# Side work of a unit in smaller pieces: reciprocal in quarters, head scaling and weight parts spread, down jobs shared out

## Chip, cores and metric

The kernel runs on one core of a Trainium2 chip. The metric is device microseconds of one execution. The kernel is one program for five engines, each with its own in-order queue: TensorE (PE, with its weight loads shown as PEld), VectorE (DVE), ScalarE (ACT), GpSimd (POOL) and SyncE (SP), the last two only issuing DMAs in the part that matters here.

## The reference

A gated mix of a linear-attention block and a bilinear feed-forward block over 2048 tokens of width 512, in float32:

```python
g = sigmoid((x * gate_w).sum(-1))
# a: 32 heads of width 16
q, k, v = x @ wqkv            # 512 x 1536
pq, pk = phi(q), phi(k)       # phi(t) = (t + 1 if t > 0 else exp(t)) + 1e-6
kv, z  = pk^T v, pk.sum(tokens)          # per head
a = (pq @ kv) / (pq . z + 1e-6) @ wo
# b: no nonlinearity, F = 1792
b = ((x @ w_gate) * (x @ w_up)) @ w_down
out = g * a + (1 - g) * b
```

## The kernel before

**Numbers in halves.** Every float32 operand of a large product is split into a high part (fp32r, a copy on ACT) and a low part (what is left, a subtraction on DVE), and a product is three matmuls (`mm3`): high x high, high x low, low x high. The split of a weight block `wr` gives `wch` (ACT) and `wcl` (DVE).

**Two passes.** The first pass (to about 95 us) computes k, phi(k) and x^T phi(k). The second, which the change touches, runs 32 *units*: two pairs of token chunks (`pair` 0 and 1, 2 x 512 tokens each) times 16 units. A unit of kind "f" makes 128 columns of gate and up together for both chunks; a unit of kind "q" makes the q of 16 heads (256 columns as two rows of 128) for both chunks. The order in a pair is f0 to f5, q0, f6 to f9, q1, f10 to f13, so q units are n = 6 and 11, and n = 22 and 27 in the second pair.

**A unit** replaces the eight 128 x 256 x 512 products of a 2 x 2 block product by seven (a Strassen form). The seven products of six matmuls each go to the four PSUM banks Y, X, R, S in the order 2 (Y), 3 (X), 4 (Y), 1 (R), 5 (X), 6 (R), 7 (S). Between them ACT and DVE combine: `m2` is Y copied by ACT; R = X - m2 (DVE); `cross[:, 0]` is Y copied by ACT; t = R + cross (DVE); S = t - X (DVE); `cross[:, 1]` is X copied by ACT. An "f" unit then multiplies the two halves on DVE (`cross`), and splits them into the *hidden* tiles `hh` (ACT) and `hl` (DVE). A "q" unit instead runs `quad` four times: exp and relu on ACT, a combine on DVE, into `phq`. m2 and t share one buffer name, so the profile calls m2 `m`.

**Side work in a unit.** A unit has places at which other work is put in the order of the program: (n, -1) after R, (n, 0) after the first `cross` copy, (n, 1) after S, (n, 2) at its end. `fill(place, k)` emits up to k *down jobs* from the list `jobs` and then all that was put at that place by `later`. A **down job** multiplies 128 tokens of two hidden tiles by their w_down blocks (six matmuls into PSUM tile `pdn`, two buffers), and DVE adds the scaled result to the output accumulator `acc`. Two f units give 8 jobs; a unit takes 1 + 1 + 2 while there are any. **Weights** of unit n+1 are split at (n, 1) by `up_weights` (three ACT copies, three DVE subtractions), followed by the negated copy for n+2 and POOL's accumulating DMA load; `w_load(n + 3)` follows the unit on SP. **down_weights** splits the unit's w_down block (`dh`, `dl`). In the first pair, 14 half tiles of the second pair's x sums are loaded, split (`cbs`) and parked in DRAM (`xpark`).

**The attention of one q unit n** is spread over later units: in n+1 the head sums (`z_parts`, `z_sum`) and the denominator (`evac` to `den`, 32 x 512); in n+2 its reciprocal in two halves (`recip`) and a DMA that spreads it to rows in DRAM (`spread`, `den<-den`); at the ends of n+2 and n+3 DMAs load four row blocks `rb` (`norm`); in n+3 and n+4 `norm2` multiplies them with phi(q) on DVE and splits them on ACT and DVE; in n+4 the folded weights kv @ wo are loaded from `wpark` (`weights`); `last` runs the head's 8 down jobs at one go, in unit n+5, or at the end of n+4 where the pair ends there.

**The turn.** After unit 15 SP reloads the x tiles from `xpark` (14 loads of 512 KB, in the order in which a unit's products use them), and PE runs all jobs that are left: 8 of f12 and f13, then 8 of q1. The same 16 end the program after unit 31; a finished tile of `out` is stored as soon as its accumulator is complete.

All PE, ACT, DVE, SP and POOL instructions named here keep their program order on their engine. Tile buffers are released in program order and waits follow from that.

Of the kernel before, what the change touches and what calls it, by code (L numbers as in the profile page):

```python
# [7 lines left out]
F32 = mybir.dt.float32  # L8
# [6 lines left out]
P = 128  # L15
# [28 lines left out]
def gated_mix(ctx: ExitStack, tc, xt, xp, x, wqkv, wq, wq_add, wo, wgu, wgu_add, wdn, gate_w, out):  # L44
# [12 lines left out]
    def act(dst, src, func=AF.Copy, **kw):  # L57
        pin(nc.scalar.activation(dst, src, func, **kw))  # L58

    def tt(dst, a, b, op):  # L60
        pin(nc.vector.tensor_tensor(dst, a, b, op=op))  # L61

    def stt(dst, a, scalar, b, op0, op1):
        pin(nc.vector.scalar_tensor_tensor(dst, a, scalar, b, op0=op0, op1=op1))  # L64

    def split(hi, lo, src, copy="act"):

        if copy == "act":
            act(hi, src)
        else:  # L70
            pin(nc.vector.tensor_copy(hi, src))
        tt(lo, src, hi.bitcast(F32), ALU.subtract)
# [72 lines left out]
            act(raws[n][:, 5:7], raws[n][:, 0:2], scale=-1.0)  # L145
            dma_add(raws[n][:, 2:7], (wgu_add if kind == "f" else wq_add)[m])

    def w_split(n, parts):
        if n < len(order):
            if n not in wcs:  # L150
                wcs[n] = [const.tile([P, 7, 2 * P], F32R, tag=f"wc{v}", name=f"wc{v}", bufs=2) for v in "hl"]
            for a, b in parts:
                split(wcs[n][0][:, a:b], wcs[n][1][:, a:b], raws[n][:, a:b])


    A1, A2, B1, B2 = range(4)
# [16 lines left out]
    with tc.tile_pool(name="p1", bufs=2, reuse_waits="tile") as p1:  # L173
# [119 lines left out]
        plan(14, lambda: w_split(0, ((0, 2), (2, 4))))  # L293
        plan(15, lambda: w_split(0, ((4, 7),)))
        plan(16, lambda: w_load(2))
        for t in range(LEAD, NT + LEAD):
            if t < NT:
# [34 lines left out]
    def later(n, place, fn):  # L332
        at.setdefault((n, place), []).append(fn)

    def fill(place, n):
        for fn in jobs[:n]:
            fn()
        del jobs[:n]
        for fn in at.pop(place, []):
            fn()  # L340

    def unit(w, n, quad):

        wh, wl = w
# [36 lines left out]
        if quad:  # L381
            quad(0, 0, bank["S"])
        else:
            hh, hl = hidden()
            act(hh[:, 1], cross[:, 1])
# [63 lines left out]
    def down_jobs(pair, group, col):  # L449

        def job(i):
            t = pair * TPP + i
            c, sl = divmod(i, CH // P)
            sl = slice(sl * P, (sl + 1) * P)
            pd = psum.tile([P, D], F32, tag="dn", name="pdn", bufs=2)
            for j, ((hh, hl), w2) in enumerate(group):
                mm3(pd, (hh[:, c, sl], hl[:, c, sl]), w2, j == 0, j == 1)
            s = col[:, t:t + 1]
            if (pair, i) not in acc:
                acc[pair, i] = p2.tile([P, D], F32, tag="acc", name="acc", bufs=8)  # L460
                act(acc[pair, i], pd, scale=s)
            else:
                a = acc[pair, i]
                stt(a, pd, s, a, ALU.mult, ALU.add)
            left[pair, i] -= 1
            if not left[pair, i]:
                to = nc.gpsimd if pair == 0 else nc.sync
                tc.keep_in_program_order(to.dma_start(out[t * P:(t + 1) * P, :], acc[pair, i]))
        return [lambda i=i: job(i) for i in range(TPP)]


    def attention(pair, j, n):
# [26 lines left out]
            den["d"] = p2.tile([4 * HB, CH], F32, tag="den", name="den")  # L499
            act(den["d"], den["p"], AF.Identity, bias=dcol[:, j, 0:1])  # L500

        def recip(half):
            sl = slice(half * CH // 2, (half + 1) * CH // 2)
            pin(nc.vector.reciprocal(den["d"][:, sl], den["d"][:, sl]))  # L504

        def spread():
# [7 lines left out]
            dma(rb, there[HB * i:HB * (i + 1)].rearrange("h j c -> (h j) c"))  # L514
            den[i] = rb

        def norm2(i):
            r, c = parts[i]
            rb = den[i]
            stt(rb, phs[r, c], EPS, rb, ALU.add, ALU.mult)  # L520
            split(group[r][0][0][:, c], group[r][0][1][:, c], rb)

        def weights():
            for r in range(2):
# [3 lines left out]
                group[r] = (group[r][0], d)  # L528

        def last():  # L530
            for fn in down_jobs(pair, [group[0], group[1]], gcol):
                fn()

        for i in range(4):
            later(n + 1, i // 2 - 1, lambda i=i: z_parts(i))
        for i in range(4):
            at.setdefault((n + 1, i // 2), []).insert(i % 2, lambda i=i: z_sum(i))
        later(n + 1, 1, evac)
        later(n + 2, -1, lambda: recip(0))
        later(n + 2, 0, lambda: recip(1))  # L540
        later(n + 2, 0, spread)
        for i, (m, place) in enumerate(((n + 3, 1), (n + 4, -1), (n + 4, 0), (n + 4, 1))):
            later(n + 2 + i // 2, 2, lambda i=i: norm(i))
            later(m, place, lambda i=i: norm2(i))
        later(n + 4, 0, weights)
        if n + 5 in (units, 2 * units):
            later(n + 4, 2, last)
        else:
            later(n + 5, 0, last)
        return quad  # L550


# [14 lines left out]

    wp_load()
    g_evac()
    later(0, 1, d_unit)  # L570
    later(1, 0, kv_unit)
    later(1, 1, lambda: wp_unit(0))
    later(1, 1, lambda: wp_unit(1))
    later(2, 0, lambda: wp_unit(2))
    later(2, 0, lambda: wp_unit(3))
    for n, (i, k) in enumerate((i, k) for i in (2, 3, 4, 1, 5, 6, 7) for k in range(2)):
        later(n, 1, lambda i=i, k=k: cb_load(i, k))
        later(n + 1, 0, lambda i=i, k=k: x_add(cb[i, k], 1, i, k))
        later(n + 2, 0, lambda i=i, k=k: cb_split(i, k))
    wdr = {}  # L580

    def d_load(n):
# [8 lines left out]
    for n, (pair, kind, m) in enumerate(order):  # L591
        entry = {}

        def down_weights(n=n, entry=entry):
            entry["d"] = down_tiles()
            split(*entry["d"], wdr.pop(n))
            d_load(n + 1)

        def up_weights(n=n):
            w_split(n + 1, ((0, 2), (2, 4), (4, 7)))  # L600
            w_add(n + 2)

        if kind == "f":
            at.setdefault((n, 0), []).insert(0, down_weights)
        at.setdefault((n, 1), []).insert(0, up_weights)
        quad = attention(pair, m, n) if kind == "q" else None
        hid = unit(wcs.pop(n), n, quad)
# [12 lines left out]
        fill((n, 2), len(jobs) if turn or n + 1 == len(order) else 0)  # L620


# [49 lines left out]
```

## Time and profile before

| | |
|---|---|
| timed runs, median of 3 | 649.72 us (648.67 to 650.14) |
| profiled execution, device time | 648.4 us |
| its span | 646.7 us |
| mean granted TensorE clock | 0.989 |
| second pass, start of unit 0 | about 95.9 us |
| end of the 16 jobs of the turn, start of unit 16 | 377.7 us |

A row of a timeline gives start, duration, engine, line, operation, the tiles written and read, shape and count; in brackets stands the engine's idle time just before it and what ended it. All helpers record one line each (52 for matmuls, 58 for ACT, 61 and 64 for DVE, 81 and 84 for DMAs), so groups are told apart by tiles. A row of waits gives who waited, for whom, total us, times, and the longest. A row of windows gives the stretch and its length, then busy time of PE, PEld, DVE, ACT and POOL with counts, the granted PE clock, the share of the DMA engines and GB/s. A row of a chain gives start, duration and work. A row of DMA issues gives size and us from issue to landing.

### The profile page before, as it was taken

How to read it: one execution, taken by the hardware profiler on the slowest of the kernel's cores; microseconds unless marked ns; L12 is line 12 of the kernel's file. 1: busy time of each engine (PE TensorE's matmuls, PEld its weight loads, DVE VectorE, ACT ScalarE, POOL GpSimd, SP SyncE). 2: the span in 40 equal slices, each digit the busy share in tenths (PEclk: the TensorE clock that was granted, in tenths of full speed). 3: DMA queues.
4: the chain of work that ended last, by engine and by line, in shares of the span. 5: the costliest groups of instructions: out<-in, count | busy, mean ns of one | idle time of the engine just before them, and what ended most of it. 6: DMA issues, size and time to landing. Idle time of an engine off the chain costs nothing.

```text
span 646.7 us, 7560 instructions
## 1 busy us (share of the span) xinstructions
PE 621.2 (96%) x2695; PEld 498.6 (77%) x2695; DVE 452.0 (70%) x693; ACT 295.4 (46%) x507; POOL 46.4 (7%) x62
## 2 busy tenths in 40 slices
PE   8999999999999899999897999999999999999997
PEld 5788887878888687787675877888887877877775
DVE  5977874555778868768778546457677786777764
ACT  2765754466456453445344025553365442553410
POOL 0011100001111100111100021000000100000000
PEclk9999999999999999999898899999999999999999
DMA  8477935578676797816986956553345763347203
GB/s 274 152 221 157 281 108 175 120 259 188 174 183 162 197 239 194 214 26 162 250 223 201 387 231 147 113 115 99 98 98 120 177 190 83 82 99 164 72 32 131
DMA packets 41926, 106.67 MB, mean 165 GB/s; under 512 B 4384, under 2 KB 6432, under 8 KB 41888
## 3 DMA queue, kind: packets, MB, share of 16 engines
q1 hardware_dynamic: 34480, 77.87, 37.6%
q0 software_dynamic: 7408, 28.32, 23.5%
q8 instruction: 21, 0.34, 0.2%
q14 instruction: 17, 0.14, 0.1%
HBM read 88.34 MB, written 17.83 MB: 164 GB/s over the span
## 4 chain that ended last, share of the span: by engine, by line
PE 77%; DVE 14%; ACT 4%; issue 2%; DMA 2%; SPq 0%; DVEq 0%
PE pdn L52 27%; PE bY L52 11%; PE bX L52 10%; PE bR L52 10%; PE gt L52 6%; PE pk L52 6%; PE bS L52 5%; DVE wcl L61 3%; ACT hh L58 3%; DVE hl L61 2%; DVE acc L64 2%; DVE rb L64 2%; DVE den L504 1%; DMA wr<-in_wgu 1%; PE pd L52 1%
## 5 line engine op out<-in xcount | busy, mean ns | idle before, releaser
L52 PE MATMUL pdn<-dh,hh 128*128 128x512 f32 x288 | 113.5, 394 | 7.8 <-ACT hh L58 7.8
L64 DVE SCALAR_TENSOR_TENSOR acc<-pdn,ocol,acc 128x512 f32<-128x512 f32 x96 | 71.7, 750 | 63.4 <-PE pdn L52 62.6
L52 PE MATMUL pdn<-dh,hl 128*128 128x512 f32 x288 | 113.5, 394 | 0.0
L52 PE MATMUL pdn<-dl,hh 128*128 128x512 f32 x288 | 113.0, 393 | 0.0
L61 DVE TENSOR_TENSOR wcl<-wr,wch 128x512 fp32r<-128x512 f32 (+1 forms) x96 | 69.8, 775 | 22.0 <-ACT wch L58 22.0
L58 ACT ACTIVATE cross<-bX 128x512 f32<-128x512 f32 x32 | 19.2, 599 | 115.8 <-DVE bS L61 115.8
L52 PEld LDWEIGHTS pdn<-dh,hh 128*128 128x128 f32 x288 | 54.7, 190 | 20.8 <-ACT hh L58 9.5
L52 PEld LDWEIGHTS pdn<-dh,hl 128*128 128x128 f32 x288 | 54.6, 189 | 13.6 <-DVE hl L61 2.4
L52 PEld LDWEIGHTS pdn<-dl,hh 128*128 128x128 f32 x288 | 54.6, 190 | 11.3
L58 ACT ACTIVATE wch<-wr 128x512 fp32r<-128x512 f32 (+1 forms) x96 | 60.2, 694 | 0.0
L58 ACT ACTIVATE hh<-cross 128x512 fp32r<-128x512 f32 x56 | 34.6, 632 | 43.1 <-DVE cross L61 43.1
L84 POOL DMA_DIRECT2D wr<-in_wgu_add x28 | 24.2, 864 | 383.1 <-ACT wr L58 334.1
L52 PE MATMUL bX<-xbh,wch 128*128 128x512 f32 x128 | 49.8, 389 | 0.0
L52 PE MATMUL bX<-xbl,wch 128*128 128x512 f32 x128 | 49.8, 389 | 0.0
L52 PE MATMUL bX<-xbh,wcl 128*128 128x512 f32 x128 | 49.8, 389 | 0.0
L58 ACT ACTIVATE cross<-bY 128x512 f32<-128x512 f32 x32 | 19.1, 596 | 59.8 <-PE bY L52 59.8
L61 DVE TENSOR_TENSOR hl<-cross,hh 128x512 fp32r<-128x512 f32 x56 | 36.6, 689 | 2.8
L64 DVE SCALAR_TENSOR_TENSOR acc<-pdn,gcol,acc 128x512 f32<-128x512 f32 x32 | 24.0, 751 | 18.9 <-PE pdn L52 18.9
L61 DVE TENSOR_TENSOR dl<-wdr,dh 128x512 fp32r<-128x512 f32 x28 | 19.2, 686 | 24.8 <-ACT dh L58 24.3
L52 PE MATMUL bR<-xc6h,wch 128*128 128x512 f32 x64 | 26.5, 414 | 6.8 <-DVE t L61 6.8
L58 ACT ACTIVATE m<-bY 128x512 f32<-128x512 f32 x32 | 18.8, 588 | 27.4 <-PE bY L52 27.2
L61 DVE TENSOR_TENSOR bR<-bX,m 128x512 f32<-128x512 f32 x32 | 22.3, 696 | 11.5 <-PE bX L52 11.2
(149 smaller groups left out, 1292.4 us busy)
## 6 DMA issues: line engine op xcount, KB each, us to landing
wr<-in_wgu SPq DMA_DIRECT2D x28, 640.0 KB, 6.2
wr<-in_wgu_add POOLq DMA_DIRECT2D x28, 640.0 KB, 7.8
wdr<-in_wdn SPq DMA_DIRECT2D x28, 256.0 KB, 2.9
xraw<-in_x SPq DMA_DIRECT2D x16, 256.0 KB, 4.7
den<-den SPq DMA_DIRECT2D x4, 1024.0 KB, 7.2
rb<-den SPq DMA_DIRECT2D x16, 256.0 KB, 6.4
cbs<-in_xp SPq DMA_DIRECT2D x14, 256.0 KB, 3.2
xtraw<-in_xt SPq DMA_DIRECT2D x12, 256.0 KB, 3.7
```

The source lines that it names most:

```text
L52: tc.keep_in_program_order(nc.tensor.matmul(*args, **kw))
L58: pin(nc.scalar.activation(dst, src, func, **kw))
L61: pin(nc.vector.tensor_tensor(dst, a, b, op=op))
L64: pin(nc.vector.scalar_tensor_tensor(dst, a, scalar, b, op0=op0, op1=op1))
L84: tc.keep_in_program_order(nc.gpsimd.dma_start(dst, src, accum_op=ALU.add))
L504: pin(nc.vector.reciprocal(den["d"][:, sl], den["d"][:, sl]))
```

## The change

A unit now has the places "e" (after R), "c" (after the first `cross` copy), "d" (before product 1), "t" (after t), "s" (between the jobs after S), "r" (before product 7) and "end".

- `recip` works on quarters of 128 columns, at "e", "c", "d" and "t" of n+2; the spreading DMA follows the last.
- `norm2` becomes `norm_high` (scale on DVE, copy on ACT) and `norm_low` (the subtraction), each at a place of its own, from (n+3, "s") and (n+3, "r") to (n+4, "s") and (n+4, "r").
- `up_weights` becomes `w_high` (three ACT copies) and `w_add`, both at once after t, and three `w_low` (DVE) around the jobs after S.
- `last` no longer runs a head's 8 jobs at one go: they go to the front of `jobs`, at the end of n+4.
- `share` gives the number of jobs at the four places of each unit: (1, 1, 1, 1), but (1, 0, 1, 1), (1, 0, 1, 0), (1, 1, 1, 0) in units 6 to 8 of a pair, (1, 2, 1, 2) in 11, (1, 1, 1, 2) in 12 and 13, and (1, 2, 1, 2) in 16 and 17. At the turn 4 jobs run, at the end of the program all.
- A list of 8 jobs begins with the second chunk (c = 1). In an f unit the ACT copy of `hh[:, 1]` comes before product 7.
- `wp_unit` 0 to 3, which fold kv into wo, move to (1, "d"), (1, "s"), (2, "e") and (2, "d"); `d_unit` is at (0, "s").

The number of instructions is the same, except for 16 reciprocals of 32 x 128 in place of 8 of 32 x 256.

```diff
-    def w_split(n, parts):
...
+    def w_high(n):
         if n < len(order):
...
+            for a, b in PARTS:
+                act(wcs[n][0][:, a:b], raws[n][:, a:b])
+
+    def w_low(n, part):
+        if n < len(order):
+            a, b = PARTS[part]
+            tt(wcs[n][1][:, a:b], raws[n][:, a:b], wcs[n][0][:, a:b].bitcast(F32), ALU.subtract)
...
+    def down(k):
+        for fn in jobs[:k]:
             fn()
+        del jobs[:k]
...
         tt(bank["R"], bank["X"], m2, ALU.subtract)
-        fill((n, -1), 1)
+        do(n, "e")
+        many = share(n)
+        down(many[0])
         product(4, "Y")
         act(cross[:, 0], bank["Y"])
-        fill((n, 0), 1)
+        do(n, "c")
+        down(many[1])
+        do(n, "d")
         product(1, "R")
         t = p2.tile([P, CH], F32, tag="t", name="t")
         tt(t, bank["R"], cross[:, 0], ALU.add)
+        w_high(n + 1)
+        w_add(n + 2)
+        do(n, "t")
         if quad:
             quad(1, 0, cross[:, 0])
         product(5, "X")
         tt(bank["S"], t, bank["X"], ALU.subtract)
         act(cross[:, 1], bank["X"])
-        fill((n, 1), 2)
+        w_low(n + 1, 0)
+        down(many[2])
+        w_low(n + 1, 1)
+        do(n, "s")
+        down(many[3])
+        w_low(n + 1, 2)
         if quad:
             quad(0, 1, cross[:, 1])
         product(6, "R")
         if quad:
             quad(1, 1, bank["R"])
         else:
+            hh, hl = hidden()
             tt(cross[:, 1], bank["R"], cross[:, 1], ALU.mult)
+            act(hh[:, 1], cross[:, 1])
+        do(n, "r")
         product(7, "S")
...
-        return [lambda i=i: job(i) for i in range(TPP)]
+        return [lambda i=i: job((i + TPP // 2) % TPP) for i in range(TPP)]
...
-        def recip(half):
-            sl = slice(half * CH // 2, (half + 1) * CH // 2)
+        def recip(part):
+            sl = slice(part * P, (part + 1) * P)
             pin(nc.vector.reciprocal(den["d"][:, sl], den["d"][:, sl]))
...
         def last():
-            for fn in down_jobs(pair, [group[0], group[1]], gcol):
-                fn()
+            jobs[:0] = down_jobs(pair, [group[0], group[1]], gcol)
...
-        fill((n, 2), len(jobs) if turn or n + 1 == len(order) else 0)
+        do(n, "end")
+        if turn or n + 1 == len(order):
+            down(4 if turn else len(jobs))
```

More of the change, by code (lines that the diff above doesn't have):

```diff
@@ L333, in later, with do, share, unit @@
         at.setdefault((n, place), []).append(fn)
-    def fill(place, n):
-        for fn in jobs[:n]:
-            fn()
-        del jobs[:n]
-        for fn in at.pop(place, []):
-            fn()
-    def unit(w, n, quad):
-        wh, wl = w
+    def do(n, place):
+        for fn in at.pop((n, place), []):
+            fn()
+    def down(k):
+        for fn in jobs[:k]:
+            fn()
+        del jobs[:k]
+    shares = {6: (1, 0, 1, 1), 7: (1, 0, 1, 0), 8: (1, 1, 1, 0), 11: (1, 2, 1, 2), 12: (1, 1, 1, 2),
+              13: (1, 1, 1, 2)}
+    early = {units: (1, 2, 1, 2), units + 1: (1, 2, 1, 2)}
+    def share(n):
+        return early.get(n) or shares.get(n % units, (1, 1, 1, 1))
+    def unit(n, quad):
+        wh, wl = wcs.pop(n)
         bank = {t: psum.tile([P, CH], F32, tag=t, name=f"b{t}") for t in "YXRS"}
@@ L383, in unit @@
         else:
-            hh, hl = hidden()
-            act(hh[:, 1], cross[:, 1])
             tt(cross[:, 0], bank["S"], cross[:, 0], ALU.mult)
@@ L515, in norm, with norm_high, norm_low @@
             den[i] = rb
-        def norm2(i):
+        def norm_high(i):
             r, c = parts[i]
-            rb = den[i]
-            stt(rb, phs[r, c], EPS, rb, ALU.add, ALU.mult)
-            split(group[r][0][0][:, c], group[r][0][1][:, c], rb)
+            stt(den[i], phs[r, c], EPS, den[i], ALU.add, ALU.mult)
+            act(group[r][0][0][:, c], den[i])
+        def norm_low(i):
+            r, c = parts[i]
+            hh, hl = group[r][0]
+            tt(hl[:, c], den[i], hh[:, c].bitcast(F32), ALU.subtract)
         def weights():
@@ L530, in last @@
         def last():
-            for fn in down_jobs(pair, [group[0], group[1]], gcol):
-                fn()
+            jobs[:0] = down_jobs(pair, [group[0], group[1]], gcol)
         for i in range(4):
-            later(n + 1, i // 2 - 1, lambda i=i: z_parts(i))
+            later(n + 1, "ec"[i // 2], lambda i=i: z_parts(i))
         for i in range(4):
[L537 to L549, printed above, removed]
+            later(n + 1, "ds"[i // 2], lambda i=i: z_sum(i))
+        later(n + 1, "r", evac)
+        for i, place in enumerate("ecdt"):
+            later(n + 2, place, lambda i=i: recip(i))
+        later(n + 2, "t", spread)
+        for i in range(4):
+            later(n + 2 + i // 2, "end", lambda i=i: norm(i))
+        for i, places in enumerate((((n + 3, "s"), (n + 3, "r")), ((n + 4, "e"), (n + 4, "c")),
+                                    ((n + 4, "d"), (n + 4, "t")), ((n + 4, "s"), (n + 4, "r")))):
+            for fn, (m, place) in zip((norm_high, norm_low), places):
+                later(m, place, lambda i=i, fn=fn: fn(i))
+        later(n + 4, "c", weights)
+        later(n + 4, "end", last)
         return quad
@@ L569, in gated_mix @@
     g_evac()
[L570 to L575, printed above, removed]
+    later(0, "s", d_unit)
+    later(1, "c", kv_unit)
+    for b, (n, place) in enumerate(((1, "d"), (1, "s"), (2, "e"), (2, "d"))):
+        later(n, place, lambda b=b: wp_unit(b))
     for n, (i, k) in enumerate((i, k) for i in (2, 3, 4, 1, 5, 6, 7) for k in range(2)):
-        later(n, 1, lambda i=i, k=k: cb_load(i, k))
-        later(n + 1, 0, lambda i=i, k=k: x_add(cb[i, k], 1, i, k))
-        later(n + 2, 0, lambda i=i, k=k: cb_split(i, k))
+        later(n, "s", lambda i=i, k=k: cb_load(i, k))
+        later(n + 1, "c", lambda i=i, k=k: x_add(cb[i, k], 1, i, k))
+        later(n + 2, "c", lambda i=i, k=k: cb_split(i, k))
     wdr = {}
@@ L597, in down_weights @@
             d_load(n + 1)
-        def up_weights(n=n):
-            w_split(n + 1, ((0, 2), (2, 4), (4, 7)))
-            w_add(n + 2)
         if kind == "f":
[L604 to L607, printed above, removed]
+            at.setdefault((n, "c"), []).insert(0, down_weights)
+        hid = unit(n, attention(pair, m, n) if kind == "q" else None)
         w_load(n + 3)
```

11 lines of the change are left out of this document (5 added, 6 removed).

## The prediction

> **What bounds the kernel now.** I read the page's busy shares first, then PE's waits, then PE's and DVE's timelines around the longest of them.
>
> ```profile
> PE 621.2 (96%) x2695; PEld 498.6 (77%) x2695; DVE 452.0 (70%) x693; ACT 295.4 (46%) x507; POOL 46.4 (7%) x62
> PE pdn L52 <- ACT hh L58: 7.8, 4, 4.1
> PE bR L52 <- DVE t L61: 6.8, 4, 2.0
> PE bY L52 <- ACT m L58: 3.3, 6, 0.8
> 200.87 1.36 PE bX L52 x6
> ```
>
> PE is the bound: it is busy nearly everywhere, and a product or a down job is 6 matmuls, 1.36 us. A unit of 7 products and 4 jobs is thus 14.96 us. What can be won is the time in which PE waits for DVE and ACT: 7.8 + 6.8 + 3.3 = 17.9 us in 14 waits. To each belongs a restart, and to the long ones a slow clock:
>
> ```profile
> 222.79 0.39 PE L52 MATMUL bX<-xbh,wcl 128*128 128x512 f32 x1
> 225.19 0.50 PE L52 MATMUL bR<-xc6h,wch 128*128 128x512 f32 x1 [2.01 <-DVE t L61]
> 225.52 0.40 PE L52 MATMUL bR<-xc6l,wch 128*128 128x512 f32 x1
> 354.13 0.80 PE L52 MATMUL pdn<-dh,hh 128*128 128x512 f32 x1 [4.14 <-ACT hh L58]
> 498.69 0.50 PE L52 MATMUL bR<-xc6h,wch 128*128 128x512 f32 x1 [1.41 <-DVE t L61]
> 225.20:229.50 4.30, 4.30 (x12) 3.40 (x13) 3.08 (x5) 2.89 (x5) 0.35 (x1) 0.60 1.01 245
> 354.20:359.20 5.00, 5.00 (x12) 3.89 (x13) 2.11 (x4) 0.00 (x0) 0.00 (x0) 0.50 1.01 275
> 499.00:503.00 4.00, 4.00 (x19) 3.12 (x18) 2.82 (x5) 2.89 (x5) 0.34 (x1) 1.00 0.90 182
> ```
>
> The steps 222.79 to 225.19 to 225.52 are 2.40 and 0.33 where 0.23 each would do: 2.27 lost for a wait shown as 2.01, so about 0.26 more for each, 3.6 for 14. After the 2.01 and 4.14 waits the granted clock (the third number from the right in the windows) is 0.60 over 4.3 us and 0.50 over 5.0: 1.7 and 2.5 us lost. After 1.41 it is 1.00. The four waits for t (6.8) can only be two of 2.0 and two of 1.4; I count 1.7 for each 2.0. Loss now: 17.9 + 3.6 + 1.7 + 1.7 + 2.5 = 27.4 us. With n the unit that makes an attention head's q, I sort it so: unit n+2 (waits for t) 6.8 + 4 x 0.26 + 3.4 = 11.2; units n+4 and after (three pdn waits, 7.8 - 4.1 = 3.7; four bY waits of 0.46) 3.7 + 1.8 + 7 x 0.26 = 7.3; the turn between the pairs (4.14 wait, its clock, and a bY wait of 0.7 in unit 17) 7.9; the like bY wait in unit 1, 1.0.
>
> **Unit n+2: the reciprocal.** DVE takes its queue in order (the last two rows are an ACT copy and one of the short bY waits):
>
> ```profile
> 219.81 1.73 DVE L504 RECIPROCAL den<-den 32x256 f32<-32x256 f32 x1
> 222.85 1.73 DVE L504 RECIPROCAL den<-den 32x256 f32<-32x256 f32 x1
> 224.52 0.62 DVE L61 TENSOR_TENSOR t<-bR,cross 128x512 f32<-128x512 f32 x1
> 249.44 0.69 DVE L61 TENSOR_TENSOR bR<-bX,m 128x512 f32<-128x512 f32 x1
> 250.04 0.74 DVE L64 SCALAR_TENSOR_TENSOR acc<-pdn,ocol,acc 128x512 f32<-128x512 f32 x1
> 250.70 0.68 DVE L64 SCALAR_TENSOR_TENSOR rb<-phq,rb 128x512 f32<-128x512 f32 x1
> 220.99 0.62 ACT L58 ACTIVATE dh<-wdr 128x512 fp32r<-128x512 f32 x1
> 607.62 0.50 PE L52 MATMUL bY<-xc4h,wch 128*128 128x512 f32 x1 [0.46 <-ACT m L58]
> ```
>
> Instructions start one after another every 0.60 (tensor_tensor), 0.66 (accumulate) and 1.67 us (reciprocal, 222.85 to 224.52). Now both halves stand ahead of t, and this unit has no job to hide them. Afterwards one quarter stands behind t, and jobs (3 in the first head's n+2, 5 in the second's) give PE cover. The trace has no 128-column reciprocal: a quarter is 0.83 (half of 1.67) to 1.73 (no shorter); I take 0.85, nearest to proportion. Count from the unit's start: X's subtraction starts at 2.9 (two products and 0.19 until the result counts); a quarter and the first accumulate bring DVE to 5.0; dl has to wait for ACT (Y's eviction at 5.6, then dh) until 6.8; cbs, quarter, accumulate, quarter: 10.3; t ends at 10.9, the last quarter at 11.7, S at 12.4. With 3 jobs PE wants t at 10.88 and S at 12.24: 0.2 lost. With 5 jobs the third job after product 5, due at 12.24, needs the PSUM buffer whose accumulate runs 12.9 to 13.65: 1.4 lost. In the second pair there is no cbs, DVE is 0.6 earlier: 0 and 0.8. So 2.4 stays of 11.2, **8.8 gained**; no wait is over 1.45, so no slow clock. At 1.73 a quarter, t comes 2.6 later in all four: some 8 lost, 3 gained.
>
> [...]
>
> **Units n+3, n+4: norm in two parts, half c=1 first.** Now a row block is scaled, split on ACT and subtracted without a pause:
>
> ```profile
> 242.78 2.15 DVE L61 TENSOR_TENSOR wcl<-wr,wch 128x512 fp32r<-128x512 f32 x3
> 244.85 0.69 DVE L64 SCALAR_TENSOR_TENSOR rb<-phq,rb 128x512 f32<-128x512 f32 x1
> 246.24 0.69 DVE L61 TENSOR_TENSOR hl<-rb,hh 128x512 fp32r<-128x512 f32 x1 [0.70 <-ACT hh L58]
> 247.45 0.68 DVE L61 TENSOR_TENSOR cross<-bS,cross 128x512 f32<-128x512 f32 x1
> 248.70 0.58 ACT L58 ACTIVATE m<-bY 128x512 f32<-128x512 f32 x1
> den<-den SPq DMA_DIRECT2D x4, 1024.0 KB, 7.2
> rb<-den SPq DMA_DIRECT2D x16, 256.0 KB, 6.4
> ```
>
> DVE idles 0.70 for ACT, and the chain cross, hh, m on two in-order queues makes the next unit's product 4 late. Unit n+4 holds 12 tensor_tensors, 3 rb, 4 accumulates and the three weight parts: 7.2 + 2.0 + 2.7 + 2.1 (wcl, 242.78 to 244.85) = 14.0 us, under PE's 14.96; with three idles of 0.70 it is 16.1, over it, and the excess becomes the waits. After the change other work stands between scaling and subtraction, and the idles go. DVE enters n+4 about 3.1 us behind its start (after n+3's hl), and 3.1 + 14.0 less the last three (1.8) + 1.8 in which dl waits for ACT puts the last cross at 17.1 to 17.8; hh and m2 take 0.6 each: m2 is ready at 19.0, 4.0 of the next unit, and product 4 is due at 4.08. The head's own jobs begin with c=1, whose parts are done; the last part is wanted five jobs later. I leave 0.8 for near misses: **6.5 gained**. What it hangs on is the rows: the last quarter ends near 11.8 of a 13.8 us unit, 7.2 and 6.4 later is 11.6 of n+3, and scaling is due at 12.3. Behind that wait stand the accumulate, the last weight part and cross, and PE waits for those.
>
> **Queues passed by the weight copies.** The three ACT copies, the negated copy and POOL's accumulating load now precede ACT's eviction of product 5 and, in q units, the first exp:
>
> ```profile
> 191.68 1.28 ACT L58 ACT_TABLE_LOAD   x1
> 195.99 1.88 ACT L58 ACTIVATE wch<-wr 128x512 fp32r<-128x512 f32 x3
> ```
>
> In unit 6, ACT after 5.6 does four copies (0.55 each from start to start, 2.2), 1.88, the table load, exp and relu (1.2), with handovers: 12.1; DVE's combine and S end at 13.3, PE wants S at 12.24: **1.1 lost**. Later q units have no table load and get S by 11.5. In f units the copies run where ACT idled: nothing, and if the 640 KB load were late, ACT's slack up to product 3 of the next unit, some 4 us, covers it. In unit 1 the spread weights remove 1.0, but wp_unit(0) now follows kv_unit directly: the mask multiply, a tensor_tensor of 0.69, and 0.3 of restart stand on PE: **0 net**.
>
> **The turn.** Now 16 jobs cover the reload of x; afterwards 4 do, and 12 go into units 16 and 17.
>
> ```profile
> 350.04 0.86 POOL L84 DMA_DIRECT2D wr<-in_wgu_add  x1 [17.07 <-ACT wr L58]
> 350.63 0.43 SPq L81 DMA_DIRECT2D xah<-xpark2h  x1
> 353.62 0.56 SPq L81 DMA_DIRECT2D xc4l<-xpark4l  x1
> 367.02 0.32 SPq L81 DMA_DIRECT2D xal<-xpark7l  x1
> xah<-xpark2h SPq DMA_DIRECT2D x1, 512.0 KB, 8.6
> xc4l<-xpark4l SPq DMA_DIRECT2D x1, 512.0 KB, 13.4
> xal<-xpark7l SPq DMA_DIRECT2D x1, 512.0 KB, 13.0
> 349.15 0.39 PE L52 MATMUL pdn<-dh,hh 128*128 128x512 f32 x1
> 377.71 0.39 PE L52 MATMUL bY<-xah,wch 128*128 128x512 f32 x1
> 364.00:368.00 4.00, 4.00 (x20) 3.30 (x19) 2.25 (x3) 0.00 (x0) 0.00 (x0) 1.00 1.03 414
> ```
>
> Unit 15 ended at 349.15, the reload was issued 1.5 later behind the weight load (which waits for DVE's last weight part), and landed in issue order: xah 8.6, xc4l 353.62 + 13.4 - 350.63 = 16.4 after the first issue. Then the DMAs ran full, 414 GB/s. Afterwards unit 15 ends earlier against DVE, and I put the issue 2.1 behind its end. So product 4 of unit 16 starts at 18.5, having done 4 jobs, two products and one job, 9.5: 9.0 lost. From there the loads outrun PE. But POOL's accumulating load, which started beside the reload, is issued some 3.5 earlier, and xah and its followers can land up to 3.3 sooner: 5.7 to 9.0. I take 7.0 of the old 7.9: **0.9 gained**.
>
> **Sum.** 8.8 + 6.5 - 1.1 + 0 + 0.9 = 15.1 off the profiled execution's 648.4 (span 646.7): 633.3, I say 633. The three timed runs' median, 649.72, is 1.3 above the profiled one; about 0.2%, 1.3 us, is also what a measurement can tell from no change.
>
> **Rivals.** *The lag stays* (0.20): rows land 1 to 2 later than 11.6 of n+3, or quarters are near 1.73; DVE enters n+4 late and waits for m2 and hh remain, half of 8.8 + 6.5: 641. For it: DVE is 14.0 of 14.96 there. Against: the removed idles.
> *The clock at the turn* (0.12): PE idles from 5.4 to 10.7 behind unit 15, longer than the 4.14 that halved the clock. If two windows as in 354 to 359 fall on PE-bound work, 2.5 to 3.4 go: 636. [...]
> *More* (0.10): reload at its early bound, and job order hides n+2's 1.4 and 0.8: 628.
> *Slower* (0.07), one place, the turn: if the fourteen loads share the rings and product 2 waits for the last (367.02 + 13.0 = 380.0, 29.4 after the first issue), unit 16 starts 31.5 behind unit 15 with 5.4 done: 26.1 lost against 7.9, 18.2 more, against 14.2 gained elsewhere: 652. It decides once product 2 starts over 27.5 behind unit 15. Against: the landings in issue order, and in the changed order each product waits for its own tile's load.
> *That the change does nothing*: the instruction order of the changed kernel has the quarters and the shared jobs, so I give it no chance; another 0.03 lies within 0.2% by chance sums.
>
> **Numbers.** Forecast 0.48 (630 to 636.5). Range 627 to 643: from the larger gain to past the staying lag; outside lie the slower case and small tails. Faster 0.48 + 0.20 + 0.12 + 0.10 = 0.90, same 0.03, slower 0.07.
>
> **What would show it.** Right: waits of PE for DVE t and ACT hh nearly gone, reciprocals near 0.85 to 0.9, one new wait of pw for kvm, one of unit 6 for S, waits of pdn for DVE acc in units 13 and 29, and PE's longest idle at the turn, for loads, 5 to 9 in all. Wrong: bY waiting for m at each n+5 (lag), unit 16 starting over 20 us behind unit 15, or PE waits that total over 15.

## The result and the profile after

The changed kernel takes 632.47 us (median of 4 runs, 631.55 to 634.54); the kernel before, timed beside it, 649.81 (4 runs, 648.67 to 650.14). The ratio is 0.9741, with a 95% interval of 0.9714 to 0.9767: 2.6% faster, 17.3 us. The forecast was 633.0 in 627 to 643, so time and sign were right. The profiled execution of the changed kernel is its longest run (634.54, span 632.8); the other three, 631.55 to 632.52, list a granted clock of 1.000 where this one has 0.995.

The busy shares and the first line of the chain that ended last, from the page of the changed kernel:

```profile
PE 617.4 (98%) x2695; PEld 499.4 (79%) x2695; DVE 449.0 (71%) x701; ACT 297.6 (47%) x507; POOL 46.4 (7%) x62
PE 90%; DVE 3%; DMA 2%; ACT 2%; issue 1%; SPq 0%; DVEq 0%; ACTq 0%
```

The work is the same (2695 matmuls); PE's share rises from 96 to 98%. PE's waits behind the first pass in the changed kernel (us in total, times, longest):

```profile
PE pdn L52 <- DVE acc L64: 3.2, 3, 1.3
PE bS L52 <- DVE bS L61: 1.0, 1, 1.0
PE bY L52 <- DMA xah<-xpark2h: 0.9, 1, 0.9
PE bR L52 <- DVE t L61: 0.8, 1, 0.8
PE pw L52 <- DVE kvm L61: 0.8, 1, 0.8
PE bY L52 <- DMA xal<-xpark2l: 0.7, 1, 0.7
PE bX L52 <- DMA xbl<-xpark3l: 0.4, 1, 0.4
```

The three rows that bounded the kernel, pdn for hh 7.8, bR for t 6.8, bY for m 3.3, are gone: the one wait for t that is left is unit 0's, not one of a unit n+2. What remains is 7.8 us in nine waits, and three of them are for the loads at the turn.

DVE's timeline in unit 8, a unit n+2 (start, duration, instruction):

```profile
218.96 0.93 DVE L536 RECIPROCAL den<-den 32x128 f32<-32x128 f32 x1
219.82 0.64 DVE L64 SCALAR_TENSOR_TENSOR acc<-pdn,ocol,acc 128x512 f32<-128x512 f32 x1
222.15 0.69 DVE L61 TENSOR_TENSOR dl<-wdr,dh 128x512 fp32r<-128x512 f32 x1 [1.69 <-ACT dh L58]
...
224.79 0.93 DVE L536 RECIPROCAL den<-den 32x128 f32<-32x128 f32 x1
225.66 0.61 DVE L61 TENSOR_TENSOR t<-bR,cross 128x512 f32<-128x512 f32 x1
```

The group row of the reciprocals, from the view of groups by shape:

```profile
L536 DVE RECIPROCAL den<-den 32x128 f32<-32x128 f32 x16 | 14.9, 930 | 0.0
```

And PE's timeline at t in unit 8 and at the jobs of units 13 and 29:

```profile
226.02 0.39 PE L52 MATMUL pdn<-dh,hl 128*128 128x512 f32 x1
226.32 0.50 PE L52 MATMUL bR<-xc6h,wch 128*128 128x512 f32 x1
...
307.22 0.39 PE L52 MATMUL pdn<-dh,hl 128*128 128x512 f32 x1
308.86 0.50 PE L52 MATMUL pdn<-dh,hh 128*128 128x512 f32 x1 [1.25 <-DVE acc L64]
...
571.25 0.39 PE L52 MATMUL pdn<-dh,hl 128*128 128x512 f32 x1
572.29 0.50 PE L52 MATMUL pdn<-dh,hh 128*128 128x512 f32 x1 [0.65 <-DVE acc L64]
```

A quarter lasts 0.93 and the next instruction starts 0.86 after it. Against the unit, t is not earlier but later: it starts 225.66 - 215.36 = 10.3 behind the start of unit 8, where it was 224.52 - 216.21 = 8.3 before. But PE now has three jobs to do until it comes: product 6, which waits for t, starts 0.30 behind the start of the last matmul of the job in front of it, 0.07 more than the usual 0.23. In units 13 and 29 the third job after product 5 waits for an accumulate; from start to start that loses 1.41 and 0.81 beyond the usual 0.23.

At the turn (PE's timeline, then SP's DMA issues and the us from issue to landing of two of them, then two windows with PE's busy time, granted clock, DMA share and GB/s):

```profile
342.99 0.39 PE L52 MATMUL pdn<-dh,hh 128*128 128x512 f32 x1
...
347.93 0.50 PE L52 MATMUL pdn<-dh,hh 128*128 128x512 f32 x1 [1.26 <-DVE acc L64]
...
351.87 0.47 PE L52 MATMUL bY<-xah,wch 128*128 128x512 f32 x1 [0.94 <-DMA xah<-xpark2h]
353.06 0.50 PE L52 MATMUL bY<-xal,wch 128*128 128x512 f32 x1 [0.71 <-DMA xal<-xpark2l]
...
360.80 0.51 PE L52 MATMUL bY<-xc4h,wch 128*128 128x512 f32 x1
```

```profile
344.04 0.33 SPq L81 DMA_DIRECT2D wr<-in_wgu  x1
344.43 0.94 SPq L81 DMA_DIRECT2D xah<-xpark2h  x1
...
347.73 0.45 SPq L81 DMA_DIRECT2D xc4l<-xpark4l  x1
xah<-xpark2h SPq DMA_DIRECT2D x1, 512.0 KB, 7.3
xc4l<-xpark4l SPq DMA_DIRECT2D x1, 512.0 KB, 10.7
```

```profile
225.20:229.50 4.30, 4.30 (x20) 1.00 0.93 194
354.20:361.00 6.80, 6.23 (x15) 0.50 1.03 411
```

The first window is that of the slow clock behind t before: it now has 1.00. The second is at the turn, 6.8 us at half clock, and costs an estimated 2 us in this one execution (634.54 against 632.42, the median of the other three).

### The profile page after: what moved, and what is told of

It reads as the page before. It is cut to its first block, busy times and chain, and to the rows that moved or that the text cites. A ratio compares the mean times of both kernels' runs of the same rounds, so it can differ in the third digit from the quotient of the medians.

```text
span 632.8 us, 7589 instructions
## 1 busy us (share of the span) xinstructions
PE 617.4 (98%) x2695; PEld 499.4 (79%) x2695; DVE 449.0 (71%) x701; ACT 297.6 (47%) x507; POOL 46.4 (7%) x62
## 4 chain that ended last, share of the span: by engine, by line
PE 90%; DVE 3%; DMA 2%; ACT 2%; issue 1%; SPq 0%; DVEq 0%; ACTq 0%
PE pdn L52 28%; PE bY L52 14%; PE bX L52 13%; PE bR L52 13%; PE bS L52 7%; PE pk L52 6%; PE gt L52 6%; DMA xbl<-xpark3l 1%; PE pd L52 1%; DVE acc L64 1%; PE pw L52 1%; PE pkv L52 1%; DVE wcl L61 1%; DMA xpark6l<-cbs 1%; ACT wch L58 0%
## 5 line engine op out<-in xcount | busy, mean ns | idle before, releaser
L61 DVE TENSOR_TENSOR wcl<-wr,wch 128x512 fp32r<-128x512 f32 (+1 forms) x96 | 72.7, 770 | 0.0
L61 DVE TENSOR_TENSOR hl<-cross,hh 128x512 fp32r<-128x512 f32 x56 | 38.2, 688 | 3.0 <-ACT hh L58 0.3
L61 DVE TENSOR_TENSOR bS<-t,bX 128x512 f32<-128x512 f32 x32 | 22.1, 690 | 9.8 <-PE bX L52 8.9
L52 PEld LDWEIGHTS bX<-xbl,wch 128*128 128x128 f32 x128 | 24.3, 190 | 6.0 <-DMA xbl<-xpark3l 0.9
```

What stands on the lines that cost most here:

```text
L52: tc.keep_in_program_order(nc.tensor.matmul(*args, **kw))
```

## Experiments: one part undone

Theory 1 is the prediction's: jobs in n+2 are PE's cover for the reciprocal, and the scaling in two parts takes the idles out of n+4. Four kernels undo one part of the change each.

**Reciprocal in halves again**, at the first two places:

```diff
-            sl = slice(part * P, (part + 1) * P)
+            sl = slice(2 * part * P, 2 * (part + 1) * P)
-        for i, place in enumerate("ecdt"):
+        for i, place in enumerate("ec"):
-        later(n + 2, "t", spread)
+        later(n + 2, "c", spread)
```

> The changed kernel with the reciprocal in two halves again (at e and c of n+2, the spreading DMA at c), all else as changed. Theory 1 (the down jobs now in unit n+2 give PE cover, the size of the reciprocal's pieces does not matter): one half more stands before t, but DVE waits for dl until 6.8 anyway, so t ends at 11.0 instead of 10.9, and S comes 0.9 earlier because no quarter follows t; the third accumulate in units 13 and 29 comes 0.7 earlier each: 1 us less than the changed kernel, 631 to 632.5. Theory 2 (quarters took the waits for t away): the waits of PE for t return, two of 2.0 with a slow clock and two of 1.4, 8 to 9 us more, 641.

Measured: 630.0 us (628.51 to 631.74; ratio to before 0.9705, 0.9674 to 0.9735). This is theory 1, and a little below its range: PE's one wait for t is unit 0's (1.1). By the medians halves are even 2.5 better than quarters, though the runs of the two overlap (up to 631.74 here, from 631.55 there); 1.3 of it is seen in the traces, where the waits of units 13 and 29 shrink from 1.41 and 0.81 to 0.77 and 0.17.

**Jobs not shared out**: one job at each place, the head's eight in one go, all jobs at the turn, as before.

```diff
-        return early.get(n) or shares.get(n % units, (1, 1, 1, 1))
+        return (1, 1, 1, 1)
-            jobs[:0] = down_jobs(pair, [group[0], group[1]], gcol)
+            for fn in down_jobs(pair, [group[0], group[1]], gcol):
+                fn()
-        later(n + 4, "end", last)
+        if n + 5 in (units, 2 * units):
+            later(n + 4, "end", last)
+        else:
+            later(n + 5, "c", last)
-        do(n, "end")
...
-            down(4 if turn else len(jobs))
+            down(len(jobs))
+        do(n, "end")
```

> The changed kernel with the jobs not shared out: 1 + 1 + 1 + 1 in a unit while there are any, a head's 8 jobs at one go in n+5 (or at the end of the pair), all jobs at the turn. The reciprocal stays in quarters. Theory 1: units n+2 have no jobs again, t ends 2.3 too late in four of them, S 0.1, two or more with a slow clock: 8 to 9 us come back; but 16 jobs cover the reload at the turn again, where the changed kernel lost 8.1, of which 7 goes, and unit 6 with 4 jobs waits 1.3 less for S: together about the time of the changed kernel, 631 to 635, with the waits at other places. Theory 2 (quarters suffice for n+2): no waits for t, and the turn's 7 won: 624 to 626. Theory 3 (sharing out is a plain gain): 640.

Measured: 637.11 us (636.79 to 638.86; 0.9819, 0.9796 to 0.9841). None of the three ranges held it. Its waits of PE, and one of three windows at half clock:

```profile
PE bR L52 <- DVE t L61: 8.0, 5, 2.0
PE pdn L52 <- ACT hh L58: 1.5, 1, 1.5
```

```profile
229.20:232.50 3.30, 3.30 (x9) 2.56 (x8) 2.83 (x6) 1.08 (x2) 0.00 (x0) 0.50 0.91 152
```

The waits for t are back as they were (2.0, 2.0, 1.4, 1.4, beside unit 0's), with the slow clock: some 11 us, 9 more than in the changed kernel. So quarters do not remove them, sharing does. That the total is only 4.6 over the changed kernel has its reason elsewhere: at the turn sixteen jobs cover the reload, and it loses some 4 less than in the profiled run of the changed kernel, and unit 6's wait for S (1.3) is not there.

**Scaling and subtraction back to back:**

```diff
-            for fn, (m, place) in zip((norm_high, norm_low), places):
-                later(m, place, lambda i=i, fn=fn: fn(i))
+            for fn in (norm_high, norm_low):
+                later(*places[0], lambda i=i, fn=fn: fn(i))
```

> The changed kernel with scale, copy and subtraction of a row block back to back again (at s of n+3, e, d and s of n+4), all else as changed. Theory 1 (the pauses of 0.70 in which DVE waits for ACT are what made it late): three pauses in n+4, m2 of the next unit is ready 2 later than 4.0, product 4 waits about 2.2 in units 11 and 27; behind units 15 and 31 the jobs with c=1 first cover it or the reload hides it: 4 to 5 us more, 636.5 to 637.5. Theory 2 (starting with c=1 is what took the waits away): 632 to 633.

Measured: 635.3 us (633.97 to 636.79; 0.9786, 0.9759 to 0.9813), 2.8 over the changed kernel, between the theories. The idle of 0.70 for ACT is back in DVE's queue, but only one wait for m came of it (0.8, unit 11); in unit 27, where DVE has no `cbs` to do in the unit before, none came. The longest wait, 2.46, was at the turn, where an accumulate stands behind unit 15's late hl, with 3.4 us of half clock after it (0.50 in 349.60:353.00).

**Weight parts in one block** behind the jobs after S:

```diff
-        w_high(n + 1)
-        w_add(n + 2)
...
-        w_low(n + 1, 0)
         down(many[2])
-        w_low(n + 1, 1)
-        do(n, "s")
         down(many[3])
-        w_low(n + 1, 2)
+        w_high(n + 1)
+        for part in range(3):
+            w_low(n + 1, part)
+        w_add(n + 2)
+        do(n, "s")
```

> The changed kernel with the weight work of unit n+1 at one place again, behind both jobs after S: three copies, three subtractions, the negated copy and the accumulating load. Theory 1: the wait for S in unit 6 (1.3) goes, the accumulate in units 13 and 29 comes 0.6 earlier (1.3 less); unit 1 waits for m2 again (1.0), n+4 gets a little later, and the accumulating load falls beside the reload again (1 to 3 more at the turn): 632 to 635. Theory 2 (the weights ahead of ACT's other work are a loss): 629 to 630.5. Theory 3 (spreading the weights is a main part of the gain): over 637.

Measured: 635.07 us (634.72 to 635.96; 0.9783, 0.976 to 0.9807), 2.6 over, just above theory 1's range. Unit 6's wait for S is gone, unit 1's wait for m is back (0.8), and the turn is worse: acc 1.8, xah 1.4, xal 0.7, then 3.4 us of half clock (0.50 in 355.40:358.80), and the granted clock of all its runs is 0.996 or 0.997.

## Experiments: one part alone on the kernel before

The four undone parts sum to 7.5 (one of them negative), not to 17.3. So parts were put alone into the kernel before.

**Quarters alone:**

```diff
-        later(n + 2, -1, lambda: recip(0))
-        later(n + 2, 0, lambda: recip(1))
-        later(n + 2, 0, spread)
+        for i, place in enumerate((-1, 0, 0, "t")):
+            later(n + 2, place, lambda i=i: recip(i))
+        later(n + 2, "t", spread)
```

> The kernel before with one edit: the reciprocal in quarters, one after X's subtraction, two behind the weights of the down projection and one behind t. Theory 1 (what removes the wait for t in unit n+2 is cover for PE, that is jobs, and not the size of the pieces): 648.5 to 651.5 us, the four waits for t stay at 2.0 and 1.4; the quarter that no longer stands ahead of t is given back, since dl then waits 0.9 for ACT's dh, as in the run with unshared jobs. Theory 2 (what stands ahead of t counts): t comes 0.7 sooner four times (2.8) and no wait is long enough to slow the clock (3.4): 643 to 645 us.

Measured: 650.85 us (649.41 to 652.28, 10 runs; 1.0023, 1.0008 to 1.0037): slightly slower than before. PE's waits, and DVE's timeline in unit 8:

```profile
PE pdn L52 <- ACT hh L58: 7.9, 4, 4.1
PE bR L52 <- DVE t L61: 7.5, 5, 2.0
PE bY L52 <- ACT m L58: 3.3, 6, 0.8
```

```profile
223.38 0.69 DVE L61 TENSOR_TENSOR dl<-wdr,dh 128x512 fp32r<-128x512 f32 x1 [0.90 <-ACT dh L58]
...
224.59 1.75 DVE L505 RECIPROCAL den<-den 32x128 f32<-32x128 f32 x2
226.26 0.61 DVE L61 TENSOR_TENSOR t<-bR,cross 128x512 f32<-128x512 f32 x1
```

The quarter taken from in front of dl is lost again there, since dl waits 0.90 for ACT: t starts 226.26 - 217.95 = 8.3 behind the start of unit 8, as it did before. Theory 1 holds.

**Sharing alone** (the head's jobs queued, half c=1 first, and the shares; reciprocal in halves, sixteen jobs at the turn):

```diff
+    shares = {6: (1, 0, 2), 7: (1, 0, 1), 8: (1, 1, 1), 11: (1, 2, 3), 12: (1, 1, 3), 13: (1, 1, 3)}
...
-        fill((n, 1), 2)
+        fill((n, 1), share(n)[2])
...
-        return [lambda i=i: job(i) for i in range(TPP)]
+        return [lambda i=i: job((i + TPP // 2) % TPP) for i in range(TPP)]
...
-            for fn in down_jobs(pair, [group[0], group[1]], gcol):
-                fn()
+            jobs[:0] = down_jobs(pair, [group[0], group[1]], gcol)
```

> The kernel before with one edit: the attention head's eight down jobs go to the front of the queue (half c=1 first) and are handed out by the changed kernel's shares, the third and fourth number together behind S; the reciprocal in halves, the scaling, the weights and the sixteen jobs at the turn stay as before. Theory 1 (cover is what counts): the four waits for t, 11.2 with their slow clock, go but for some 2, the rest stays: 639 to 642 us. Theory 2 (DVE is the lag, and jobs moved into n+2 only move the waits to n+3 to n+5, where scaling and weights still stand back to back): 645 to 649 us.

Measured: 636.92 us (636.03 to 637.75; 0.9806, 0.9773 to 0.9839): 12.7 off, more than theory 1 had. PE's waits:

```profile
PE bY L52 <- ACT m L58: 5.1, 8, 1.2
PE pdn L52 <- DVE acc L64: 3.2, 3, 2.2
PE bR L52 <- DVE t L61: 0.7, 2, 0.6
```

In the units n+2 no wait for t but one of 0.16 is left (the other 0.6 is unit 0's), and the mean granted clock of the profiled execution is 0.996 instead of 0.989: some 10 of the 11.2. The lag of n+4 stays, as waits for m (5.1 in 8, of which 1.5 are those of units 1 and 17), so that term hardly moves. The turn loses about 6 instead of 7.9.

**Scaling in two parts alone** (and c=1 first):

```diff
-            split(group[r][0][0][:, c], group[r][0][1][:, c], rb)
+            act(group[r][0][0][:, c], den[i])
...
+            tt(hl[:, c], den[i], hh[:, c].bitcast(F32), ALU.subtract)
...
+        for i, places in enumerate((((n + 3, 1), (n + 3, "r")), ((n + 4, -1), (n + 4, 0)),
+                                    ((n + 4, 0), (n + 4, "t")), ((n + 4, 1), (n + 4, "r")))):
```

> The kernel before with one edit: the scaling of a head's row block and its subtraction stand apart (other work of DVE between them), and the head's eight jobs, still done in one go, begin with half c=1. Theory 1 (the prediction's step: the idles of 0.70 in unit n+4 set the waits for m and hh there and after): 6.5 less than before, 642.5 to 644 us. Theory 2 (the lag in n+4 and after is mostly want of cover, as the run with sharing alone suggests, and the step is worth what its undoing cost in the changed kernel, 2.8): 646 to 648 us.

Measured: 636.63 us (635.96 to 638.98; 0.9813, 0.9793 to 0.9833): 12.6 off, twice what theory 1 had. Its waits of PE, and two windows of 3.40 us, about the length of the half-clock stretches in the kernel before (3.41, see the last section):

```profile
PE bR L52 <- DVE t L61: 7.2, 5, 2.0
PE pdn L52 <- ACT hh L58: 1.7, 1, 1.7
PE bY L52 <- ACT m L58: 1.4, 2, 0.8
```

```profile
225.30:228.70 3.40, 1.54 (x7) 1.28 (x8) 2.50 (x3) 0.77 (x2) 0.00 (x0) 1.00 0.99 280
228.70:232.10 3.40, 3.40 (x16) 2.67 (x15) 3.02 (x5) 2.29 (x5) 0.86 (x1) 1.00 0.99 199
```

In n+4 and after, under 1 of the 7.3 is left: the prediction's 6.5 is right for that place. The rest comes from two places that theory 1 did not count. At the turn the wait for hh is 1.7 instead of 4.1, and no slow clock follows (1.00 in 348.00:351.40; about 4). And the four waits for t are as long as before, but their slow clock (3.4) does not come (1.00 in 228.70:232.10 and in 312.40:315.80); why was not shown. With the waits unchanged, that 3.4 is not counted as work of the scaling. Beginning with c=1 was not run by itself: at the turn of the kernel before, ACT copies the two halves of hh back to back (1.23 us for both) and the first job waited for the second, so an estimated 0.6 of the 4 belongs to it; in n+4 the run with sharing alone also begins with c=1 and kept its lag.

## Experiments: the turn, and a better version

**Halves, and eight jobs at the turn:**

```diff
-    early = {units: (1, 2, 1, 2), units + 1: (1, 2, 1, 2)}
+    early = {}
-            down(4 if turn else len(jobs))
+            down(8 if turn else len(jobs))
```

> The changed kernel with the reciprocal in halves and with eight jobs at the turn instead of four, units 16 and 17 then taking one at each place. Theory 1 (what the turn loses is the reload's landing, which four jobs do not cover): the waits for the tiles of x at the turn, some 2.5 with restarts in the run with halves (630.0), go, and the slow clock cannot come: 627 to 628 us. Theory 2 (the turn is set by DVE, the third job's accumulate behind hl, 1.35 to 2.5, and jobs taken from units 16 and 17 bring waits there): 629.5 to 631 us.

Measured: 627.22 us (627.07 to 628.1; 0.9661, 0.9635 to 0.9687). Theory 1: its trace shows no wait for a tile of x at the turn, and only the third job's accumulate (1.3) and 0.6 from start to start in the first job, one of whose weight tiles (`dl<-wpark3l`) landed late, are left there.

**Quarters, and eight jobs at the turn** (the last edit alone):

> The changed kernel with eight jobs at the turn and units 16 and 17 at one job a place; the reciprocal stays in quarters. Beside the run with halves and eight jobs (627.2) it differs by the size of the pieces alone. Theory 1 (quarters cost only what the waits of pdn for acc in units 13 and 29 are longer, 0.65 each): 628.3 to 629 us. Theory 2 (quarters cost the whole 2.5 by which the run with halves was under the changed kernel): 629.5 to 630 us.

Its four times are 629.02, 629.27, 685.28 (granted clock 0.852) and 3537.29; only the first two can be compared. They are 1.9 over halves, 1.3 of it in units 13 and 29 (1.42 and 0.81 against 0.77 and 0.17). They lie between the two ranges, nearer to theory 1.

**Four more waits taken away:**

```diff
-              13: (1, 1, 1, 2)}
+              13: (1, 2, 1, 1)}
-    for b, (n, place) in enumerate(((1, "d"), (1, "s"), (2, "e"), (2, "d"))):
+    for b, (n, place) in enumerate(((1, "t"), (1, "s"), (2, "e"), (2, "d"))):
+        if quad:
+            quad(1, 0, cross[:, 0])
         w_high(n + 1)
         w_add(n + 2)
         do(n, "t")
-        if quad:
-            quad(1, 0, cross[:, 0])
...
             tt(hl[:, 1], cross[:, 1], hh[:, 1].bitcast(F32), ALU.subtract)
+            if n + 1 == units:
+                do(n, "end")
+                down(2)
-            down(8 if turn else len(jobs))
+            down(6 if turn else len(jobs))
```

> As the run before it (halves, eight jobs at the turn), and four of the waits seen in the changed kernel taken away: unit 13 takes its jobs (1, 2, 1, 1) instead of (1, 1, 1, 2) (0.8 and 0.2 in the run with halves), the first wp product follows t instead of kvm (1.0), in a q unit exp and relu of Y come ahead of the weight copies (unit 6, 1.3), and two of the eight jobs at the turn, with their accumulates, stand ahead of unit 15's second hl (1.5). If each wait is a loss of its own, these sum to some 4.5: 622 to 624 us. If PE's covers are shared out and a wait removed returns at the next place, 626 to 628 us.

Measured: 623.12 us (622.06 to 629.53; 0.9616, 0.9562 to 0.967). The waits for S in unit 6, for kvm, and for acc in units 13 and 29 are gone from its trace, and that at the turn is 0.4. Each was a loss of its own. The run of 629.53 lists a clock of 0.994.

**Unit 0's down weights loaded earlier** (`d_load(0)` ahead of `wp_load()`):

> As the run with halves, eight jobs at the turn and four waits taken away (623.1), and the load of unit 0's down weights is issued ahead of those of wv and wo. If unit 0's wait for t (1.0 with its restart) comes from this load: 621.5 to 622.5 us. If it comes from the order on ACT or DVE: 623 us, unchanged.

Measured: 626.14 us (623.31 to 629.11, 6 runs; 0.9645, 0.9615 to 0.9674). Neither expectation held. The wait for t in unit 0 is gone from the trace, so it came from this load, but no time is gained; the profiled run (623.31) has other waits in its place: the wait for the last tile of x is 1.6 instead of 1.1 and that for the first tiles of the first pass 1.6 instead of 1.1. Three of six runs lie at 627.5 to 629.1, with a clock of 0.994 to 0.997; no trace was taken of those, and why they are slower is open.

**Twelve jobs at the turn**, without that earlier load:

```diff
-    early = {}
+    early = {units: (1, 0, 1, 0), units + 1: (1, 0, 1, 0)}
-            down(6 if turn else len(jobs))
+            down(10 if turn else len(jobs))
```

> As the run with halves, eight jobs at the turn and four waits taken away (623.1, one of its four times at 629.5), with twelve jobs at the turn, the first two of them ahead of unit 15's second hl; units 16 and 17 then have two each. Theory 1 (the last wait at the turn, 1.1 to 1.6 for the last tile of x in unit 16's product 7, and the times near 628 to 629 at a lower granted clock both come from the reload's landing): the wait goes, 621 to 622.5 us, and no time stands over 625. Theory 2 (the times near 628 come from somewhere else, and units 16 and 17 with two jobs each get waits for m2): 623 to 625 us with single times up to 629.

Measured: 623.18 us (622.04 to 624.9, 6 runs; 0.9598, 0.9573 to 0.9623), the version to keep: 4.0% under before, 9.3 under the changed kernel. Its busy row and PE's waits behind the first pass:

```profile
PE 611.5 (98%) x2695; PEld 496.3 (80%) x2695; DVE 450.1 (72%) x693; ACT 297.8 (48%) x507; POOL 46.0 (7%) x62
```

```profile
PE bR L52 <- DVE t L61: 1.1, 1, 1.1
...
PE pdn L52 <- DVE acc L64: 0.6, 1, 0.6
...
PE bS L52 <- DMA xal<-xpark7l: 0.3, 1, 0.3
```

The wait for the last tile is 0.3 instead of 1.1, and no run stands over 625, as theory 1 has it; the time itself stays at 623, above its range and in theory 2's, and units 16 and 17 show no wait for m. That the times near 629 came from the reload is thus likely, not shown. Three waits after the first pass are left in this list, 2.0 us.

## Why the prediction was right

By its own steps, in the profiled executions (loss from start to start beyond 0.23); the lines are DVE's in unit 6 of the changed kernel, for the third step:

```profile
198.32 0.69 DVE L64 SCALAR_TENSOR_TENSOR phq<-ex,phq 128x512 f32<-128x512 f32 x1 [3.98 <-ACT phq L58]
198.93 0.69 DVE L61 TENSOR_TENSOR bS<-t,bX 128x512 f32<-128x512 f32 x1
```

- **Unit n+2.** 2.4 should stay of 11.2; 0.1 in unit 8, 1.4 in 13, none in 24, 0.8 in 29 did: 2.3. Gained 8.9 where 8.8 was said. The sum's times came too: in unit 8 t ends 10.9 and S 12.4 behind the unit's start, as said. The quarter was put at 0.85 and takes 0.86 from its start to the next. By their durations the eight more instructions add 14.9 - 8 x 1.73 = 1.1 us, but little of it reached DVE's queue: from start to start two quarters take 1.67 in a row (quarters alone, 224.59 to 226.26) or 2 x 0.86, where a half takes 1.67, so at most 8 x 0.05 = 0.4 us. The forecast for these units as a whole was right, but one claim in the change's favour was not tested there and fell in the runs: the quarters are no part of the gain; alone they cost 1.3, and with everything else in place 1.9 to 2.5, of which 1.3 is traced to the accumulates in units 13 and 29.
- **Units n+4 and after.** 0.8 should stay of 7.3; 0.3 did (608.92 to 609.42, the last jobs). Gained 7.0 where 6.5 was said. The scaling in two parts, with c=1 first, cleared that place alone as well.
- **Queues passed by the weight copies.** 1.1 lost was said for unit 6; it is 1.3. DVE's combine waits for exp and relu, which stand behind the copies and the table load (1.28), and S behind the combine (the lines above). Putting exp and relu ahead of the copies was among the four edits that left no such wait.
- **Units 0 and 1.** Unit 1's wait for m went (1.0) and the wait for kvm came (0.8 and restart), as said. Unit 0's wait for t (0.8) was not foreseen; the kernels with the old order have it too in some executions (0.35 to 0.66).
- **The turn: the step that was mis-sized.** 7.0 was said (5.7 to 9.0) against 7.9 before: 0.9 gained. Product 4 of unit 16 starts 360.80 - 342.99 = 17.8 behind unit 15's end, 8.3 more than its 9.5 of work: 0.4 lost. The loads came near the early end of what was said: the first was issued 1.4 behind the end, not 2.1, and xc4l landed 347.73 + 10.7 - 342.99 = 15.4 behind it. Not in the sum was the half clock (2.0), a rival with 0.12; it came in the profiled run and, by their granted clock of 1.000, not in the other three, where an estimated 6.3 remain. The accumulate behind unit 15's hl (1.4) was not in the sum either and cost nothing here, since PE then had to wait for xah, landed at 344.43 + 7.3 = 351.7, in any case; it shows in the run with eight jobs (1.3). One sign named beforehand failed: PE's longest idle at the turn is 1.26, for that accumulate, and its waits for loads are 2.1 in all, not 5 to 9, though the time lost there is of that size. What the step did not see is that 7.9 was the wrong thing to compare with: once the lag is gone, sixteen jobs at the turn lose 3.7 (the run with scaling alone). Moving twelve of them away spent an estimated 6.3 - 3.7 = 2.6 without the slow clock; the run with eight jobs got 2.8 back.
- **The sum.** 15.1 were said; 13.9 came between the profiled executions, though the first pass took 1.2 longer in that of the changed kernel (unit 0 starts at 97.08 instead of 95.87). From unit 2 on 15.7 were gained, of which the steps above account for 14.2; the other 1.5 lie in short restarts that were not sorted one by one. Between the medians it is 17.3. The 15.1 were taken off the one profiled execution (648.4); off the median of 649.8 they give 634.7. That the median meets 633 to 0.5 is partly luck: the runs without the slow clock at the turn are those that make it.

Sharing and scaling alone gain 12.7 and 12.6, but not 25 together. In n+2 and n+4 they do not overlap but for the slow clock (3.4). At the turn, each alone ends part of the wait for hh (1.9 and 4.2 of 7.9 gained) while the sixteen jobs still cover the reload, and the whole change gives that up.

## What to carry to other kernels

A wait of the bounding engine for a side job goes when the bounding engine has other work to do at that place, and smaller pieces alone did not do it: look for queued work to put there before cutting an instruction up. Undo each part and also do each part alone: their difference showed a step (the jobs moved away from the turn) that cost part of what the others had won. When a bound moves, price each step against what the place would lose after the others, not against its loss before.

## What the hardware showed

**Half clock came in stretches of 3.41 and 6.83 us.** Two windows of the kernel before show one of them (busy times of PE, PEld, DVE, ACT, POOL, then granted clock):

```profile
222.63:226.05 3.42, 1.41 (x7) 0.85 (x6) 3.20 (x4) 0.08 (x1) 0.00 (x0) 1.00 0.77 232
226.05:229.46 3.41, 3.41 (x10) 2.64 (x9) 2.34 (x4) 2.80 (x5) 0.31 (x1) 0.50 1.00 208
```

PE is busy for 1.41 of the first window and gets half speed in the next. In this execution the granted clock is 0.50 in 226.05:229.46, in 314.79:318.21 and in 352.34:359.17, and 1.00 between them and from there to 645.80; the second and the third stretch begin 88.74 and 126.29 us behind the first, 26 and 37 times 3.41. In the changed kernel it is 0.50 in 354.21:361.03, and 1.00 from 9.50 to 354.20 and from 361.04 to 634.00.

PE's idle time in the 3.41 us ahead of these stretches is 2.01, 2.01 and 2.35 in the kernel before and, with several waits, 1.65 in the changed one. In the kernel before, 1.41 in 495.70:499.11 and 1.45 in 618.58:621.99 were followed by 1.00. In the run with scaling alone the same wait of 2.01 ends at 227.16; of 225.30:228.70 PE is busy for 1.54, idle for 1.86, and the next 3.40 us have 1.00. So the idle time in such a window does not settle it alone: 1.65 was followed by half clock and 1.86 was not, and the same wait of 2.01 cost 1.7 us more or nothing. What decides between the two was not shown.

**The first pass varies.** In the profiled execution of the kernel before, the first matmuls of `pk` start 0.23 us apart from 5.75 to 8.05 us; in that of the changed kernel they start 0.43 apart from 5.88 to 9.30 us and 0.23 apart from 9.61 on. Unit 0 then started at 95.87 and at 97.08. So 1.2 us between these two executions arise before unit 0, ahead of the units that the change touches; which of the two starts a run gets is open.
